# Summing u by channel block, and starting the channel MLP's first two feature groups side by side

## The chip, the cores and the metric

The kernel runs on one core of a Trainium2 chip. The metric is the device time of one execution in microseconds (us), as the median of several runs. A core has TensorE (matmuls), VectorE, ScalarE and GpSimd (elementwise work) and SyncE (which only issues DMAs here); each works through its own queue in order, and semaphores join the queues. In the rows they are PE (with PEld for the loading of weights), DVE, ACT, POOL and SP. TensorE writes into PSUM, eight banks of 512 float32 words per partition, which VectorE and ScalarE read.

## What is computed

Three stages follow one another: a gated linear attention, a mixing over the sequence with a channel MLP, and a second MLP with a spatial gate. The change lies at the start of the middle stage, for the first of four batches:

```python
def _moe_ref(x, U, V, w_ch1, w_ch2):          # x: (4, 768, 384)
    xt = x.transpose(0, 2, 1)
    h = xt @ U @ V                            # U: 768 x 32, V: 32 x 768
    u = x + h.transpose(0, 2, 1)
    ch = np.maximum(u @ w_ch1, 0.0) @ w_ch2   # 384 -> 1536 -> 384
    return (u + ch)
```

All is float32. Products run in a faster float32 mode on operands split into a high part and a low part (the rest): `high x high + low x high + high x low`.

## The kernel before

**Tiles.** A batch's u is held channels first: 384 channels are three blocks of 128 (index m or k, KE = 3), 768 positions are two blocks of 384 (index blk, NB = 2, TB = 384). A block's tuple is `(t, hi, lo)`: u in float32, its rounded copy and the rest. The 1536 hidden features are 12 groups of 128 (index f). A weight tile `w[f]` holds the high and the low parts of both matrices for one group.

**From x to u.** For each channel block m, `Mix.product` multiplies the transposed x with U into one PSUM bank, and `keep` writes it to columns m of `stk`: ScalarE copies 96 rows (line 1242), VectorE subtracts for the 32 rows of rests (line 1243). `mix_sum` then multiplies `stk` (block m) with V on TensorE (line 318), VectorE adds the result to t (line 322), ScalarE makes hi (line 323), and `rest` makes lo (line 252). In `first_batch` of the kernel before the order is: the three products with their keeps, `weights.add()`, all six sums with their hi copies, four products that fill time (`busy`, line 945), six rests (block 0, m = 0 on GpSimd, five on VectorE), and `weights.finish(1)`.

**The channel MLP.** For features 0 to 4 the two position blocks run side by side (`side_by_side`). The up product of a group and a block is nine matmuls (wh x uh, wh x ul, wl x uh, three channel blocks each, line 380) into a bank; ScalarE takes the ReLU to h (line 387, line 409 for the first group) and VectorE the rest hl = max(bank, 0) - h (`rest_of_h`, line 368). So the bank is read twice, and last by VectorE. `up_both` makes the first group for both blocks: six high products of block 0, six of block 1, then three low products of each (line 400). The down product (`down_group`, lines 287 to 289) is three times three matmuls into three accumulators; it runs two groups behind (`flush(2)`), so after the up products of (f0, block 0), (f0, block 1) and (f1, block 0) comes the down product of (f0, block 0), then the up product of (f1, block 1), then the down product of (f0, block 1). Within a down product the rest of the last h is put into VectorE's queue between the first and the second accumulator (`if m == 1: self.rest_of_h()`).

**Banks.** Banks are taken in turn by name: "acc" is banks 0 to 2, "mm" 3 and 4, "x" 5 to 7. Up products use "mm"; the accumulators of block 0 are three "acc", those of block 1 three "x"; the mixing products use "x"; the sums of u use "acc" for block 0 and "x" for block 1. A bank that is taken again waits for the last reader of what it held.

**Weights.** Features are loaded as 64-bit words and taken apart: two VectorE operations for the high word (lines 237 and 240), a scaling of the low word on ScalarE (line 232), an add of both (line 247, on GpSimd for features 0 and 1, on VectorE after them), a high part by ScalarE (line 791) and a low part by VectorE (line 252). These steps are spread by hand: `pull()` is called at fixed points of the MLP, and `FIRST_STEPS` says at which pull a step is queued ("f": the next half of the splitting, "b": the beginning of the next feature). At the 5th pull, inside `up_both`, the low part of f1 is queued; at the 6th feature 2 begins; at the 13th, inside the up product of (f1, block 1), "fbf" queues the high part of f2, the three operations of f3 and the low part of f2. The need for f1 (`need(2)`) queues the loads of pairs 5 and 6.

Of the kernel before, what the change touches and what calls it, by code (L numbers as in the profile page):

```python
# [36 lines left out]
F32 = mybir.dt.float32  # L37
# [3 lines left out]
AF = mybir.ActivationFunctionType  # L41
# [21 lines left out]
KE = E // 128  # L63
TB = 384
NB = S // TB
# [7 lines left out]
FIRST = (0, 5, 8, 10, 12)  # L73
# [27 lines left out]
def gla_mixer_gating_kernel(ctx: ExitStack, tc: tile.TileContext, akq, v, v2, vT, u, v3, w12, w_in, wsT, b_sp, w_out, out):  # L101
    nc = tc.nc
# [38 lines left out]
    class Stage:  # L141
# [38 lines left out]
        def high(self, room=None):  # L180

            place, words, t, n, wide, finish = self.loaded.pop(0)
            if wide and not place:
                t = (room or self.narrow())[0 : words.shape[0], 0:n]
            if wide:
                high_part(words, t)
            self.raised.append((place, words, t, wide, finish, self.scaled > 0))
            self.scaled = max(0, self.scaled - 1)
# [40 lines left out]
    def low_part(words):  # L229

        low = words.rearrange("p (n w) -> p n w", w=2)[:, :, 0]
        nc.scalar.activation(out=low, in_=low, func=AF.Copy, scale=2.0**-29)
# [17 lines left out]
    def rest(out, x, hi, engine=nc.gpsimd):  # L250

        engine.tensor_tensor(out=out, in0=x, in1=hi.bitcast(F32), op=ALU.subtract)  # L252
# [58 lines left out]
        )  # L311
        yield

    def mix_sum(g, block, blk, m, stk, psp, tag, engine=nc.gpsimd):

        t, hi, lo = block
        pt = psp.tile([128, 512], F32, "ps_h", tag)
        nc.tensor.matmul(
            out=pt[:, 0:TB], lhsT=stk[:, m * 128 : (m + 1) * 128], rhs=g["vs"][0 : stk.shape[0], blk * TB : (blk + 1) * TB],
            start=True, stop=True,  # L320
        )
        nc.vector.tensor_tensor(out=t[:, m, :], in0=pt[:, 0:TB], in1=t[:, m, :], op=ALU.add)
        nc.scalar.activation(out=hi[:, m, :], in_=t[:, m, :], func=AF.Copy)
        if engine:
            rest(lo[:, m, :], t[:, m, :], hi[:, m, :], engine)

    def mix_sum_steps(g, us, stk, up, psp, tag, blocks, parts=None):

# [7 lines left out]
    class ChannelMlp:  # L336
# [3 lines left out]
            self.wts, self.hp, self.psp, self.pull, self.need = wts, hp, psp, pull, need  # L340
            self.behind, self.h, self.accs, self.held = [], None, {}, False

        def side_by_side(self, b, blocks, f0, f1, tags):

            self.held = True
            for f in range(f0, f1):
                self.need(f + 1)
                for blk, h in enumerate(self.up_both(blocks, f) if f == f0 else (None, None)):
                    h = h or self.up_group(blocks[blk], f)
                    self.behind.append((b, blk, blocks[blk], f, h, f == f0, f == f1 - 1, tags[blk]))  # L350
                    self.flush(2)

# [16 lines left out]
                    out=hl, in0=ps[:, 0:TB], scalar=0.0, in1=h.bitcast(F32), op0=ALU.max, op1=ALU.subtract  # L369
                )  # L370

        def up_group(self, block, f):
            t, uh, ul = block
            w = self.wts
            ps = self.psp.tile([128, 512], F32, name="ps_1", tag="mm")

            wh, wl = w[f][:, 0], w[f][:, 1]
            parts = [(x, k) for x in ((wh, uh), (wh, ul), (wl, uh)) for k in range(KE)]
            for i, ((wx, ux), k) in enumerate(parts):
                nc.tensor.matmul(  # L380
                    out=ps[:, 0:TB], lhsT=wx[:, k * 128 : (k + 1) * 128], rhs=ux[:, k, :], start=i == 0, stop=i == len(parts) - 1
                )
                if i % 3 == 2 and i < len(parts) - 1:
                    self.pull()
            h = self.hp.tile([128, TB], F32R, name="h", tag="h", bufs=3)
            hl = self.hp.tile([128, TB], F32R, name="hl", tag="hl", bufs=3)
            nc.scalar.activation(out=h, in_=ps[:, 0:TB], func=AF.Relu)  # L387
            self.h = ps, h, hl
            return h, hl

        def up_both(self, blocks, f):
            w = self.wts
            wh, wl = w[f][:, 0], w[f][:, 1]
            both = [self.psp.tile([128, 512], F32, name="ps_1", tag="mm") for _ in blocks]

            for ends in (False, True):
                for (t, uh, ul), ps in zip(blocks, both):
                    parts = [(wh, ul, k) for k in range(KE)] if ends else [(wx, uh, k) for wx in (wh, wl) for k in range(KE)]
                    for i, (wx, ux, k) in enumerate(parts):
                        nc.tensor.matmul(  # L400
                            out=ps[:, 0:TB], lhsT=wx[:, k * 128 : (k + 1) * 128], rhs=ux[:, k, :],
                            start=i == 0 and not ends, stop=ends and i == KE - 1,
                        )
                    self.pull()
            hs = []
            for ps in both:
                h = self.hp.tile([128, TB], F32R, name="h", tag="h", bufs=3)
                hl = self.hp.tile([128, TB], F32R, name="hl", tag="hl", bufs=3)
                nc.scalar.activation(out=h, in_=ps[:, 0:TB], func=AF.Relu)
                self.h = ps, h, hl  # L410
                self.rest_of_h()
                hs.append((h, hl))
                if len(hs) == 1:
                    self.pull()
            return hs
# [391 lines left out]
    with ExitStack() as fast:  # L807
# [26 lines left out]
        ps = Ps(psp)  # L834
# [107 lines left out]
        def busy(n, bank):  # L942

            for _ in range(n):
                nc.tensor.matmul(out=bank[:, 512 - C : 512], lhsT=g["ident"], rhs=g["ident"], start=True, stop=True)

        class Pair:
# [77 lines left out]
            def keep(self):  # L1025

                after, self.w = self.after, states
                r0, r1 = slice(0, HW), slice(HW, 2 * HW)
                nc.scalar.activation(out=self.w[r0, :, 0, :], in_=after[r0, :, 0 : NCH - 1].rearrange("p e c -> p c e"), func=AF.Copy)
                nc.scalar.activation(out=self.w[r1, :, 1, :].rearrange("p c e -> p e c"), in_=after[r1, :, 0 : NCH - 1], func=AF.Copy)  # L1030
# [179 lines left out]
        class Mix:  # L1210
# [27 lines left out]
                return gp  # L1238

            def keep(self, gp):  # L1240
                o = slice(self.m * 128, (self.m + 1) * 128)
                nc.scalar.activation(out=self.stk[:, o], in_=gp[0 : 3 * R, 0:128], func=AF.Copy)
                nc.vector.tensor_tensor(
                    out=self.stk[R : 2 * R, o], in0=gp[R : 2 * R, 0:128], in1=self.stk[R : 2 * R, o].bitcast(F32), op=ALU.subtract
                )
# [157 lines left out]
        N_SMALL = 2  # L1403
# [12 lines left out]
        def first_batch(blocks):  # L1416
# [22 lines left out]
                mixes[m].take(pt[1], engine, room[1][:, m])  # L1439

            def summed(blk, m):
                mix_sum(g, blocks[blk], blk, m, stk, ps, ("acc", "x")[blk], None)

            for n in range(NP - 1):
                ahead = prepare(n + 1)
# [26 lines left out]
            narrow = [up.pool.tile([128, KE * TB], U32, name="narrow", tag=x) for x in ("uh0", "ul0")]  # L1472
            low_part(weights.loaded[0][1])
            low_part(weights.loaded[1][1])
            weights.scaled = N_SMALL + 1
            weights.high(narrow[0])
            weights.high(narrow[1])
            for _ in range(N_SMALL):
# [27 lines left out]
            weights.finish(1)  # L1506
            gp = mixes[1].product()
            mixes[1].keep(gp)
            blocks += [(us[blk], *up.parts()) for blk in range(NB)]
            gp = mixes[2].product()  # L1510
            mixes[2].keep(gp)
            weights.add()
            for blk, m in ((0, 0), (0, 1), (1, 0), (0, 2), (1, 1), (1, 2)):
                summed(blk, m)
            busy(4, ps.tile([128, 512], F32, "ps_w", "mm"))
            for blk in range(NB):
                t, hi, lo = blocks[blk]
                for m in range(KE):
                    rest(lo[:, m, :], t[:, m, :], hi[:, m, :], nc.gpsimd if blk == m == 0 else nc.vector)
            weights.finish(1)  # L1520
            yield
            load_pair(5)
            load_pair(6)
            next(ahead)
            yield

        blocks = []
        rest_of_first = first_batch(blocks)
        next(rest_of_first)
        nxt = []  # L1530
# [71 lines left out]
        for b in range(B):  # L1602
            if b == 0:
                n_steps = N_STEPS + N_AHEAD
            elif b + 1 < B:
                nxt = []
                steps, n_steps = attend(b + 1, nxt), N_STEPS + (2 if b > 0 else 0)
            else:
                ap_stack.close()
                gp = fast.enter_context(tc.tile_pool(name="gp", bufs=1, side="right"))  # L1610
                wts = gating_weights(gp)
                gating = Stage(gp, gating_items(wts), adders=range(NF1))
                steps = gating_steps()
            pulls, done = 0, 0
            groups = int(NB * NF1 * 2 * KE * (0.95 if b == 0 else 0.9))
            if b == 0:

                mlp.side_by_side(b, blocks, *FIRST[0:2], ("acc", "x"))
                for f0, f1 in zip(FIRST[1:-1], FIRST[2:]):
                    for blk in range(NB):  # L1620
                        mlp.block(b, blk, blocks[blk], f0, f1)
            else:
                for blk in range(NB):
                    mlp.block(b, blk, blocks[blk])
            drain(steps)
            blocks = nxt
# [184 lines left out]
```

## Time and profile before

| | us |
|---|---|
| median of 3 runs | 673.27 (673.02 to 673.37) |
| the profiled execution | 672.58 |
| its span, first to last instruction | 670.9 |
| TensorE busy | 657.1 (98%) |
| VectorE busy | 425.2 (63%) |
| ScalarE busy | 305.9 (46%) |
| GpSimd busy | 146.3 (22%) |

Times in the rows are from the start of the span. A row of the timeline is one instruction or several of one kind in a row (x and a number): start, length from the first's start to the last's end, engine, line, output and inputs, and in brackets the idle time of the engine before it with what ended it. Matmuls overlap, so a row of matmuls is longer than their spacing. The region of the change is 42 to 60 us.

### The profile page before, as it was taken

The numbers are of one execution on the slowest core, as the hardware profiler recorded it, in microseconds if no ns is written. First come the engines' busy times: TensorE is split into PE (matmuls) and PEld (weight loads), VectorE is DVE, ScalarE is ACT, GpSimd is POOL, SyncE is SP. The second block draws the span as 40 slices with busy tenths as digits, with TensorE's granted clock in tenths as the row PEclk, the third lists the DMA queues.
The fourth block names the chain that finished last, engine by engine and source line by source line (L and its number), as shares of the span: only waits on it lengthen the run. The fifth ranks groups of instructions, "written<-read, shape, count | busy, mean of one in ns | idle before, by whom it ended". The sixth has DMA issues, their size and how long they took to land.

```text
span 670.9 us, 13771 instructions
## 1 busy us (share of the span) xinstructions
PE 657.1 (98%) x5644; PEld 625.2 (93%) x5644; DVE 425.2 (63%) x813; ACT 305.9 (46%) x599; POOL 146.3 (22%) x138
## 2 busy tenths in 40 slices
PE   7999999999999999999999999999999999999996
PEld 6889999799999999999999999899999989999996
DVE  7989999867566336565327787586384356537541
ACT  3985467565455335554323444343344233334321
POOL 4530111133211131220120000306401620540041
PEclk9999999999999999999999999999999999999999
DMA  8799115562556502602023455401120202110011
GB/s 332 259 358 239 23 35 114 105 128 88 119 102 137 102 0 61 118 10 76 27 71 93 118 163 156 130 0 36 37 68 4 71 1 71 37 36 35 1 37 41
DMA packets 24039, 61.02 MB, mean 91 GB/s; under 512 B 3232, under 2 KB 13344, under 8 KB 22688
## 3 DMA queue, kind: packets, MB, share of 16 engines
q1 hardware_dynamic: 23968, 60.06, 32.7%
q8 instruction: 46, 0.75, 0.4%
q14 instruction: 25, 0.20, 0.1%
HBM read 47.47 MB, written 9.44 MB: 85 GB/s over the span
## 4 chain that ended last, share of the span: by engine, by line
PE 83%; DVE 11%; ACT 3%; issue 2%; DMA 0%; DVEq 0%; ACTq 0%
PE banks L380 19%; PE banks L287 18%; PE banks L288 18%; PE banks L289 18%; PE banks L1109 2%; DVE fw L933 2%; DVE bw L920 2%; PE banks L1008 1%; DVE narrow L240 1%; PE banks L980 1%; PE banks L964 1%; DVE narrow L247 1%; PE banks L1219 1%; DVE w L252 1%; PE banks L1235 1%
## 5 line engine op out<-in xcount | busy, mean ns | idle before, releaser
L380 PE MATMUL banks<-partuh,w 128*128 128x384 f32 x564 | 130.6, 339 | 1.4 <-DVE hl L368 1.2
L380 PEld LDWEIGHTS banks<-partuh,w 128*128 128x128 f32 x564 | 99.3, 188 | 3.1 <-DVE hl L368 1.8
L287 PE MATMUL banks<-h,w 128*128 128x384 f32 x288 | 98.0, 340 | 0.2
L289 PE MATMUL banks<-hl,w 128*128 128x384 f32 x288 | 96.4, 335 | 0.0
L288 PE MATMUL banks<-h,w 128*128 128x384 f32 x288 | 96.4, 335 | 0.0
L368 DVE SCALAR_TENSOR_TENSOR hl<-banks,h 128x384 fp32r<-128x384 f32 x96 | 52.7, 549 | 52.8 <-ACT h L387 52.2
L387 ACT ACTIVATE h<-banks 128x384 fp32r<-128x384 f32 x94 | 45.6, 487 | 76.9 <-PE banks L380 76.7
L252 POOL TENSOR_TENSOR partul<-ub,partuh 128x384 fp32r<-128x384 f32 x43 | 43.2, 1029 | 136.5 <-ACT partuh L457 84.1
L252 POOL TENSOR_TENSOR room<-room 128x384 fp32r<-128x384 f32 x32 | 32.5, 1017 | 163.5 <-ACT room L600 163.2
L380 PE MATMUL banks<-partul,w 128*128 128x384 f32 x282 | 66.0, 341 | 0.0
L287 PEld LDWEIGHTS banks<-h,w 128*128 128x128 f32 x288 | 54.0, 188 | 1.6 <-issue 0.8
L288 PEld LDWEIGHTS banks<-h,w 128*128 128x128 f32 x288 | 54.1, 188 | 0.0
L289 PEld LDWEIGHTS banks<-hl,w 128*128 128x128 f32 x288 | 54.1, 188 | 0.0
L909 POOL TENSOR_TENSOR akq<-akq,fw 128x768 f32<-128x768 f32 x13 | 22.5, 1731 | 135.0 <-DVE fw L933 86.6
L380 PEld LDWEIGHTS banks<-partul,w 128*128 128x128 f32 x282 | 49.2, 188 | 0.8
L600 ACT ACTIVATE room<-room 128x384 fp32r<-128x384 f32 x32 | 16.8, 525 | 66.8 <-DVE room L598 66.8
L252 DVE TENSOR_TENSOR vl<-vt,vh 128x512 fp32r<-128x512 f32 (+1 forms) x48 | 26.6, 616 | 20.7 <-ACT vh L505 20.7
L909 POOL TENSOR_TENSOR akq<-akq,bw 128x768 f32<-128x768 f32 x11 | 18.6, 1688 | 65.1 <-DVE bw L920 65.1
L288 PE MATMUL banks<-partuh,winl 128*128 128x384 f32 x96 | 32.4, 338 | 0.0
L289 PE MATMUL banks<-partul,winh 128*128 128x384 f32 x96 | 32.4, 338 | 0.0
L287 PE MATMUL banks<-partuh,winh 128*128 128x384 f32 x96 | 32.4, 338 | 0.0
L289 PE MATMUL banks<-woutl,room 128*128 128x384 f32 x96 | 32.3, 336 | 0.0
(256 smaller groups left out, 1495.9 us busy)
## 6 DMA issues: line engine op xcount, KB each, us to landing
akq<-in_akq SPq DMA_DIRECT2D x24, 434.4 KB, 7.5
bits<-in_w SPq DMA_DIRECT2D x12, 768.0 KB, 11.3
x2d<-ub SPq DMA_DIRECT2D x8, 576.0 KB, 3.3
ub<-x2d SPq DMA_DIRECT2D x8, 576.0 KB, 4.2
out_y<-room SPq DMA_DIRECT2D x24, 192.0 KB, 1.9
v<-in_v SPq DMA_DIRECT2D x15, 288.0 KB, 8.1
words<-in_wsT SPq DMA_DIRECT2D x7, 576.0 KB, 3.9
words<-in_w_in SPq DMA_DIRECT2D x8, 384.0 KB, 3.2
```

Of the source, the lines that this page charges most:

```text
L252: engine.tensor_tensor(out=out, in0=x, in1=hi.bitcast(F32), op=ALU.subtract)
L287: nc.tensor.matmul(out=ps, lhsT=wh, rhs=xh, start=first, stop=False, skip_group_check=more)
L288: nc.tensor.matmul(out=ps, lhsT=wl, rhs=xh, start=False, stop=False, skip_group_check=more)
L289: nc.tensor.matmul(out=ps, lhsT=wh, rhs=xl, start=False, stop=last, skip_group_check=more)
L368: nc.vector.scalar_tensor_tensor(out=hl, in0=ps[:, 0:TB], scalar=0.0, in1=h.bitcast(F32), op0=ALU.max, op1=ALU.subtract)
L380: nc.tensor.matmul(out=ps[:, 0:TB], lhsT=wx[:, k * 128 : (k + 1) * 128], rhs=ux[:, k, :], start=i == 0, stop=i == len(parts) - 1)
L387: nc.scalar.activation(out=h, in_=ps[:, 0:TB], func=AF.Relu)
L600: nc.scalar.activation(out=hi, in_=x, func=AF.Copy)
L909: engine.tensor_tensor(out=chunks(x)[:, c], in0=chunks(x)[:, c], in1=chunks(by)[:, c, 1:CW], op=ALU.mult)
L920: nc.vector.tensor_tensor_scan(out=bw[:, ::-1], data0=a[:, 1 : AW + 1][:, ::-1], data1=ends[:, ::-1], initial=0.0, op0=ALU.mult, op1=ALU.max)
L933: nc.vector.tensor_tensor_scan(out=fw, data0=a[:, 0:AW], data1=starts, initial=0.0, op0=ALU.mult, op1=ALU.max)
L1109: nc.tensor.matmul(out=self.py[HW * h : HW * h + D, x, j * CH : (j + 1) * CH], lhsT=vw[:, h, c, :], rhs=self.sms[h][:, t], start=True, sto ...
```

## The change

The sums of u are split into their steps (`mix_add`, `raised` for hi, `lowered` for lo). In `first_batch` the scaling and the add for feature 1 move ahead; the sums for channel block 0 of both position blocks are queued ahead of the third mixing product, and those for block 1 behind it, around the two halves of its keep. The sums for channel block 2, their hi copies, the splitting of feature 1's high part and five rests become `last_sums`, which `up_both` calls after its first two matmuls. `up_both` goes by channel block, high and low weights of each, and between the low products of block 0 and of block 1 it makes the first three matmuls (wh x uh) of feature 1 for both position blocks, into two more banks, named "x"; `up_group` for feature 1 then adds the other six. The four products that filled time are gone.

```diff
+    def mix_add(g, block, blk, m, stk, psp, tag):
+        t = block[0]
         pt = psp.tile([128, 512], F32, "ps_h", tag)
...
         nc.vector.tensor_tensor(out=t[:, m, :], in0=pt[:, 0:TB], in1=t[:, m, :], op=ALU.add)
...
-                for blk, h in enumerate(self.up_both(blocks, f) if f == f0 else (None, None)):
-                    h = h or self.up_group(blocks[blk], f)
+                hs, begun = [None] * NB, [None] * NB
+                if f == f0:
+                    hs = self.up_both(blocks, f, last_sums)
+                elif f == f0 + 1:
+                    begun = self.begun
+                for blk in range(NB):
+                    h = hs[blk] or self.up_group(blocks[blk], f, begun[blk])
...
-        def up_group(self, block, f):
+        def up_group(self, block, f, begun=None):
...
-            ps = self.psp.tile([128, 512], F32, name="ps_1", tag="mm")
+            ps = begun or self.psp.tile([128, 512], F32, name="ps_1", tag="mm")
...
+                if i >= KE or not begun:
...
+        def up_both(self, blocks, f, last_sums):
+            both, self.begun = ([self.psp.tile([128, 512], F32, name="ps_1", tag=x) for _ in blocks] for x in ("mm", "x"))
...
+            high(0, 0)
+            last_sums()
+            high(1, 0)
+            for k in range(1, KE):
+                for blk in range(NB):
+                    high(blk, k)
+                self.pull()
+            low(0)
+            self.pull()
+            for blk in range(NB):
+                for k in range(KE):
+                    nc.tensor.matmul(
+                        out=self.begun[blk][:, 0:TB], lhsT=self.wts[f + 1][:, 0, k * 128 : (k + 1) * 128], rhs=blocks[blk][1][:, k, :],
+                        start=k == 0, stop=False,
+                    )
+            low(1)
+            self.pull()
...
             mixes[1].keep(gp)
+            low_part(weights.raised[0][1])
+            weights.add()
             blocks += [(us[blk], *up.parts()) for blk in range(NB)]
+            summed(0, 0)
+            summed(1, 0)
             gp = mixes[2].product()
-            mixes[2].keep(gp)
-            weights.add()
-            for blk, m in ((0, 0), (0, 1), (1, 0), (0, 2), (1, 1), (1, 2)):
-                summed(blk, m)
-            busy(4, ps.tile([128, 512], F32, "ps_w", "mm"))
...
+            raised(0, 0)
+            mixes[2].keep_high(gp)
+            summed(0, 1)
+            mixes[2].keep_rest(gp)
+            summed(1, 1)
+            lowered(0, 0)
+            for blk, m in ((1, 0), (0, 1), (1, 1)):
+                raised(blk, m)
+
+            def last_sums():
+                for blk in range(NB):
+                    summed(blk, KE - 1)
+                for blk in range(NB):
+                    raised(blk, KE - 1)
+                weights.finish(1)
+                for blk, m in ((0, 1), (0, 2), (1, 0), (1, 1), (1, 2)):
+                    lowered(blk, m)
+
+            junction.append(last_sums)
             yield
```

## Rows read from the trace of the kernel before

**Rows 1.** The page's totals: busy us, share of the span, instructions of each engine
```profile
PE 657.1 (98%) x5644; PEld 625.2 (93%) x5644; DVE 425.2 (63%) x813; ACT 305.9 (46%) x599; POOL 146.3 (22%) x138
```

**Rows 2.** Busy us (instructions) of each engine by stretch, then clock, DMA share, GB/s
```profile
59.40:122.50 63.10, 61.09 (x768) 56.78 (x766) 62.01 (x99) 36.95 (x65) 5.09 (x3) 1.00 0.43 82
128.00:665.00 537.00, 536.54 (x4152) 517.16 (x4149) 307.24 (x633) 223.09 (x443) 117.68 (x107) 1.00 0.26 69
```

**Rows 3.** VectorE's waits from 43.9 to 122.5 us: total, times, longest
```profile
DVE hl L368 <- ACT h L387: 0.9, 1, 0.9
```

**Rows 4.** The chain of waits, 50 to 175 us: start, length, what
```profile
57.19 0.88 DVE w L252
58.12 0.81 PE banks L380 x3
58.95 0.50 ACT h L387
...
127.05 0.29 DVE stk L1243
127.48 0.85 PE banks L964 x6
```

**Rows 5.** The timeline of VectorE, 41 to 60 us
```profile
42.70 0.28 DVE L1243 TENSOR_TENSOR stk<-banks,stk 32x128 fp32r<-32x128 f32 x1
43.81 0.28 DVE L1243 TENSOR_TENSOR stk<-banks,stk 32x128 fp32r<-32x128 f32 x1 [0.83 <-ACT stk L1242]
44.13 2.88 DVE L322 TENSOR_TENSOR ub<-banks,ub 128x384 f32<-128x384 f32 x6
46.93 2.84 DVE L252 TENSOR_TENSOR partul<-ub,partuh 128x384 fp32r<-128x384 f32 x5
49.83 0.56 DVE L368 SCALAR_TENSOR_TENSOR hl<-banks,h 128x384 fp32r<-128x384 f32 x1
...
51.17 0.55 DVE L368 SCALAR_TENSOR_TENSOR hl<-banks,h 128x384 fp32r<-128x384 f32 x1
...
54.19 0.55 DVE L368 SCALAR_TENSOR_TENSOR hl<-banks,h 128x384 fp32r<-128x384 f32 x1
...
57.98 0.55 DVE L368 SCALAR_TENSOR_TENSOR hl<-banks,h 128x384 fp32r<-128x384 f32 x1
59.47 0.56 DVE L368 SCALAR_TENSOR_TENSOR hl<-banks,h 128x384 fp32r<-128x384 f32 x1 [0.94 <-ACT h L387]
```

**Rows 6.** Line 252 from 46 to 50 us: shortest, median, longest in ns
```profile
L252 DVE TENSOR_TENSOR partul<-ub,partuh x5: 544/544/967, 46.9 to 49.2; 128x384 fp32r<-128x384 f32 x5
```

**Rows 7.** The timeline of GpSimd, 41 to 60 us
```profile
44.65 1.86 POOL L247 TENSOR_TENSOR narrow<-narrow,bits 128x768 uint32<-128x768 uint32 x1 [5.99 <-ACT bits L232]
46.47 1.01 POOL L252 TENSOR_TENSOR partul<-ub,partuh 128x384 fp32r<-128x384 f32 x1
```

**Rows 8.** The timeline of ScalarE, 41 to 60 us
```profile
43.68 0.89 ACT L232 ACTIVATE bits<-bits 128x768 uint32<-128x768 uint32 x1
44.77 2.80 ACT L323 ACTIVATE partuh<-ub 128x384 fp32r<-128x384 f32 x6 [0.19 <-ACT bits L232]
```

**Rows 9.** The timeline of TensorE, 43 to 60 us
```profile
44.78 1.05 PE L945 MATMUL banks<-ident 128*128 128x128 f32 x8
...
46.74 2.01 PE L400 MATMUL banks<-partuh,w 128*128 128x384 f32 x10 [0.53 <-ACT partuh L323]
...
50.44 0.79 PE L380 MATMUL banks<-partuh,w 128*128 128x384 f32 x3 [0.18 <-DVE hl L368]
...
56.79 0.68 PE L380 MATMUL banks<-partuh,w 128*128 128x384 f32 x3
57.31 0.68 PE L380 MATMUL banks<-partul,w 128*128 128x384 f32 x3
```

**Rows 10.** TensorE's first matmuls, and the stretch behind its last one (clock 0.93)
```profile
1.43 4.43 PE L945 MATMUL banks<-ident 128*128 128x128 f32 x24 [1.43 <-POOL ident masks.py:199]
...
666.00:670.90 4.90, 0.00 (x0) 0.00 (x0) 0.00 (x0) 0.00 (x0) 0.00 (x0) 0.93 0.16 50
```

More of the change, by code (lines that the diff above doesn't have):

```diff
@@ L312, in mix_tile_steps @@
         yield
-    def mix_sum(g, block, blk, m, stk, psp, tag, engine=nc.gpsimd):
-        t, hi, lo = block
+    def mix_add(g, block, blk, m, stk, psp, tag):
+        t = block[0]
         pt = psp.tile([128, 512], F32, "ps_h", tag)
@@ L322, in mix_sum @@
         nc.vector.tensor_tensor(out=t[:, m, :], in0=pt[:, 0:TB], in1=t[:, m, :], op=ALU.add)
+    def mix_sum(g, block, blk, m, stk, psp, tag):
+        t, hi, lo = block
+        mix_add(g, block, blk, m, stk, psp, tag)
         nc.scalar.activation(out=hi[:, m, :], in_=t[:, m, :], func=AF.Copy)
-        if engine:
-            rest(lo[:, m, :], t[:, m, :], hi[:, m, :], engine)
+        rest(lo[:, m, :], t[:, m, :], hi[:, m, :])
     def mix_sum_steps(g, us, stk, up, psp, tag, blocks, parts=None):
@@ L341, in __init__, with side_by_side @@
             self.behind, self.h, self.accs, self.held = [], None, {}, False
-        def side_by_side(self, b, blocks, f0, f1, tags):
+        def side_by_side(self, b, blocks, f0, f1, tags, last_sums):
             self.held = True
@@ L379, in up_group @@
             for i, ((wx, ux), k) in enumerate(parts):
-                nc.tensor.matmul(
-                    out=ps[:, 0:TB], lhsT=wx[:, k * 128 : (k + 1) * 128], rhs=ux[:, k, :], start=i == 0, stop=i == len(parts) - 1
-                )
+                if i >= KE or not begun:
+                    nc.tensor.matmul(
+                        out=ps[:, 0:TB], lhsT=wx[:, k * 128 : (k + 1) * 128], rhs=ux[:, k, :], start=i == 0, stop=i == len(parts) - 1
+                    )
                 if i % 3 == 2 and i < len(parts) - 1:
@@ L389, in up_group, with high, low @@
             return h, hl
[L391 to L404, printed above, removed]
+        def up_both(self, blocks, f, last_sums):
+            both, self.begun = ([self.psp.tile([128, 512], F32, name="ps_1", tag=x) for _ in blocks] for x in ("mm", "x"))
+            def high(blk, k):
+                for i in range(2):
+                    nc.tensor.matmul(
+                        out=both[blk][:, 0:TB], lhsT=self.wts[f][:, i, k * 128 : (k + 1) * 128], rhs=blocks[blk][1][:, k, :],
+                        start=k == i == 0, stop=False,
+                    )
+            def low(blk):
+                for k in range(KE):
+                    nc.tensor.matmul(
+                        out=both[blk][:, 0:TB], lhsT=self.wts[f][:, 0, k * 128 : (k + 1) * 128], rhs=blocks[blk][2][:, k, :],
+                        start=False, stop=k == KE - 1,
+                    )
+            high(0, 0)
[8 more added lines that the diff above has]
+            for blk in range(NB):
+                for k in range(KE):
+                    nc.tensor.matmul(
+                        out=self.begun[blk][:, 0:TB], lhsT=self.wts[f + 1][:, 0, k * 128 : (k + 1) * 128], rhs=blocks[blk][1][:, k, :],
+                        start=k == 0, stop=False,
+                    )
+            low(1)
+            self.pull()
             hs = []
@@ L1240, in keep, with keep_high, keep_rest @@
             def keep(self, gp):
+                self.keep_high(gp)
+                self.keep_rest(gp)
+            def keep_high(self, gp):
                 o = slice(self.m * 128, (self.m + 1) * 128)
                 nc.scalar.activation(out=self.stk[:, o], in_=gp[0 : 3 * R, 0:128], func=AF.Copy)
+            def keep_rest(self, gp):
+                o = slice(self.m * 128, (self.m + 1) * 128)
                 nc.vector.tensor_tensor(
@@ L1441, in summed, with raised, lowered @@
             def summed(blk, m):
-                mix_sum(g, blocks[blk], blk, m, stk, ps, ("acc", "x")[blk], None)
+                mix_add(g, blocks[blk], blk, m, stk, ps, ("acc", "x")[blk])
+            def raised(blk, m):
+                t, hi, lo = blocks[blk]
+                nc.scalar.activation(out=hi[:, m, :], in_=t[:, m, :], func=AF.Copy)
+            def lowered(blk, m):
+                t, hi, lo = blocks[blk]
+                rest(lo[:, m, :], t[:, m, :], hi[:, m, :], nc.gpsimd if blk == m == 0 else nc.vector)
             for n in range(NP - 1):
@@ L1474, in first_batch @@
             low_part(weights.loaded[1][1])
-            weights.scaled = N_SMALL + 1
+            weights.scaled = N_SMALL + 2
             weights.high(narrow[0])
@@ L1508, in first_batch @@
             mixes[1].keep(gp)
+            low_part(weights.raised[0][1])
+            weights.add()
             blocks += [(us[blk], *up.parts()) for blk in range(NB)]
+            summed(0, 0)
+            summed(1, 0)
             gp = mixes[2].product()
-            mixes[2].keep(gp)
-            weights.add()
-            for blk, m in ((0, 0), (0, 1), (1, 0), (0, 2), (1, 1), (1, 2)):
-                summed(blk, m)
-            busy(4, ps.tile([128, 512], F32, "ps_w", "mm"))
[L1516 to L1520, printed above, removed]
+            raised(0, 0)
[15 more added lines that the diff above has]
+            junction.append(last_sums)
             yield
@@ L1525, in first_batch @@
             yield
-        blocks = []
+        blocks, junction = [], []
         rest_of_first = first_batch(blocks)
@@ L1616, in gla_mixer_gating_kernel @@
             if b == 0:
-                mlp.side_by_side(b, blocks, *FIRST[0:2], ("acc", "x"))
+                mlp.side_by_side(b, blocks, *FIRST[0:2], ("acc", "x"), junction.pop())
                 for f0, f1 in zip(FIRST[1:-1], FIRST[2:]):
```

## The prediction

> **What bounds the kernel now.** I read the engine totals first: TensorE is busy for 98% of the span, VectorE for 63% [rows 1]. Shares of the whole span say little about one place, so I cut the span into stretches. From 128 us on TensorE is busy 536.54 of 537.00 us: nothing there can take up a delay or add to a gain, and whatever stands at 128 us is carried to the end. Between 59.4 and 122.5 us it is VectorE that never rests: 62.01 of 63.10 us [rows 2]. Its list of waits from 43.9 to 122.5 us has only one on another engine after the sums, 0.9 us for one ReLU [rows 3]. The chain of waits says where these two meet: at 58.07 us the low half of feature group 2's weights is done, TensorE goes on 0.05 later, and the ReLU of that group follows at 58.95; at 127.48 TensorE goes on again right behind a VectorE operation [rows 4]. So the question for this change is one number: how much earlier or later VectorE begins the rest of h of group 2, block 0, which stands at 59.47 us now [rows 5]. Everything behind that is a queue without idle time, on VectorE first and on TensorE then, and shifts as a whole.
>
> I write f0, f1, f2 for feature groups and b0, b1 for blocks.
>
> **Part 1, the sums.** Now VectorE idles 0.83 us ahead of the last rest for stk (43.81), since the third product is summed before anything else is added; six adds take 2.80 from 44.13 to 46.93; five rests of u take 2.77 up to 49.70; then come hl of f0 b0 (49.83), f1's low weights and hl of f0 b1 (51.17) [rows 5]. In the new order:
> The first two sums need only the first block of stk and go ahead of the third product. The first add can follow the rest at 42.70 as closely as 44.13 follows 43.81, by 0.32: 43.02, which is 1.11 earlier. But that third rest (0.32) now lies between the adds. The add of (0,1) must wait for its matmul behind the third product, an estimated 0.09. The sum of (1,2) gets the bank of (1,1), because two of the three banks "x" are by then set aside for the begun products of f1; it waits for that add, about 0.12. So the adds end at 43.02 + 2.80 + 0.32 + 0.21 = 46.35, against 46.93: of 1.11 us, 0.58 are left.
> The five rests: their rows read 0.544 us for most and 0.967 for one [rows 6], the first, which ran while GpSimd's rest (46.47 to 47.48) did [rows 7]. GpSimd's add for f1 waits now for ScalarE's scaling at 43.68 [rows 8]; this moves ahead of the third product, behind the second keep, whose rest stands at 42.70, so to about 42.4, and GpSimd's two operations (1.86 and 1.01) end near 46.2, before the first rest of VectorE. Five at 0.47 each from 46.35 end at 48.70, 1.00 earlier than now.
> The Trainium skill has the rule for it (SBUF — State Buffer, section "Who interferes with whom"): a VectorE instruction with two SBUF inputs and a GpSimd instruction that reads SBUF exclude each other, and the adds, with one input in PSUM, are exempt. The trace agrees: the six adds ran under GpSimd's 1.86 us at one pace, 2.80 for all, the first rest did not keep its 0.544. Without that rule the first rest would stay at 0.97, and the sum below would be 1.86 instead of 1.72.
>
> **Part 2, the first products.** TensorE takes f0 by channel block, so it starts before the last sums, but its last pair of high products needs the copy of u (1,2), whose add ends at 46.45; the copy, about half a us (six in 2.80 [rows 8]), ends at 47.02. From 47.10 come two products, three of b0's low part, six begun ones of f1 and three of b1's low part, 0.173 apart (a group of three is 0.52 behind the last [rows 9]), 0.28 behind the first after a wait: the last one starts at 49.46 and ends at 49.79. f1's high weights, next on ScalarE behind that copy, are there at about 47.8, ahead of the begun six at 48.07. The six begun products are only moved, they take TensorE time that it lost before to waits (0.53 us at 46.74, 0.18 at 50.44 [rows 9]); they delay b1's ReLU by 1.04 us where it might have come sooner. ReLU 0.49, and hl of f0 b1 starts at 50.35 instead of 51.17. So up to here VectorE is **0.82 us** ahead. Bounds: VectorE's own queue without a single wait would have it 1.36 ahead (43.02, six adds, 0.32, five rests, hl 0.47, weights 0.87: 49.81); if half of the waits above are twice as long, 0.5.
> The four idle-filling products (1.05 us, eight rows [rows 9]) lie in a wait of TensorE and cost nothing when removed; the wait behind them was for a copy of u. ScalarE's scaling, moved, ends near 43.3, before the third product does (43.83), so the keep behind it waits for nothing new; without that cover it would cost 0.9. No DMA is moved: the loads of pairs 5 and 6 stay at the need for f1. The pulls of the first group stay five, so every step of the list by pulls keeps its place in the queues of ScalarE and VectorE.
>
> **Part 3, the banks.** This is where I expect the loss. Block 1's three accumulators take the three banks "x" in turn, the next after begun f1 b0, begun f1 b1, sum (1,2): so accumulator 0 falls on the bank of f1 b0, **accumulator 1 on the bank of f1 b1**. That bank is read by the ReLU and by hl of f1 b1. The first down product of b1 (f0) comes right behind the up product of f1 b1, and hl of f1 b1 stands in VectorE's queue behind all that the 13th pull puts there: f3's three operations and f2's low weights. In the trace it runs at 57.98, 6.81 us after hl of f0 b1 [rows 5], and all of that is in between still. So it starts at 50.35 + 6.81 = 57.16, ends at 57.71, and TensorE may write accumulator 1 at 57.77. Today these accumulators find free banks, and f1's h in the two "mm" banks is not written over until f2. That TensorE does wait for such a read is in the trace: the up product of f1 b0 at 50.44 stood 0.18 for the hl of f0 b0 on the same bank [rows 9].
> TensorE gets there much sooner: f1 b0's six remaining products end at 51.06 (its low weights are ready at 50.2), down f0 b0 nine, up f1 b1 six, then accumulator 0 from 53.98 (it waits for hl of f1 b0, 53.92): it is done with it at 54.8 and stands for some **3 us**. Behind the wait are queued two thirds of that down product (6 matmuls) and the up product of f2 b0 (9), which before were almost done by then. Fifteen matmuls after a stall take 0.81 + 4 × 0.52 = 2.89 us [rows 4, 9]: 57.77 + 2.89 = 60.66 for the end of f2 b0, against 58.93. VectorE has nothing to do meanwhile, because the next thing in its queue is hl of f2 b0. So this hl comes 1.73 later.
> In one line: the end of f2 b0 is 58.53 + 0.05 + 2.89 = 61.47 less what VectorE gains up to hl of f1 b1, against 58.93 now: **shift = 2.54 − gain**. With 0.82 it is +1.72 us; with the bounds 1.36 and 0.5, +1.2 to +2.0. There is no way for the gain to reach 2.54: VectorE's queue alone allows 1.36.
>
> **Sum.** The profiled execution spans 670.9 us and took 672.58, 0.69 below the median of the runs, 673.27. Shifted: 674.3 for such an execution, **675.0** for the median. A measurement of this kernel can tell about 0.2%, 1.35 us, from no change.
>
> **Rivals.**
> (a) The bank wait does not decide (the accumulators find other banks, or hl of f1 b1 is out before 54.8). Then TensorE arrives early at f2's low weights, which VectorE ends 0.82 sooner than 58.07, and all shifts by −0.8: **672.45**, not slower. For it: the wait can't be seen in the trace of before, it follows from counting banks. Against: the count leaves no other bank, and it decides as soon as f3's three operations stand ahead of that hl.
> (b) The delay is partly given back. VectorE idles 1.09 of 63.10 us up to 122.5 [rows 2]; if all of it were slack, +0.6 would be left: **673.9**. Against: the list of waits [rows 3] shows none of them as a wait for another engine; gaps between dependent operations stay.
> (c) TensorE's clock falls in the new idle stretch. The granted clock was at its upper level (2.4 GHz, 1.00) through all waits of the body; behind the last matmul it fell only late in the stretch of 666 to 670.9 us without work (mean 0.93) [rows 10]. Getting back cost about 1.6 us at the start: 24 products in 4.43 us [rows 10], where eight take 1.05 later [rows 9], about 0.111 apart with a tail of 0.16, so that 24 would take 2.83. Result 675.0 + 1.6 = **676.6**. Against: the wait here is some 3 us, shorter than the stretch at the end in which the level held at first.
> The Trainium skill (TensorE: Matmul & The Clock Gate, section "Why this matters for your kernels") warns against leaving TensorE idle between bursts of matmuls, since the clock can go back to its half rate. By that rule (c) would be the result; the trace of before has no idle stretch of such a length inside the body, so it can't say.
>
> **How the numbers follow.** Forecast 0.66, (a) 0.13, (b) 0.13, (c) 0.08. Of the forecast's range (674.5 to 675.3) nearly all lies above 674.62, the bound for slower; some 0.1 may be just below. Slower: 0.56 + 0.08 = 0.64; within: 0.10 + 0.13 + 0.08 = 0.31; faster only if (a) comes with twice the gain: 0.05. The range 673.3 to 676.2 takes in the forecast with its bounds and (b); (a) and (c) stay out.
>
> **What would show it.** In the changed profile: the first add of u starts near 43.0; TensorE has one wait of about 3 us between 54 and 58 us, on a down product of h, ended by VectorE's hl; VectorE idles some 3.4 us ahead of the next hl near 61.2; from there every operation stands 1.7 us later, to the end. I am wrong if that wait is under 1 us, if it is ended by something else, or if hl of f2 b0 starts before 60 us.

## The result

| | median us | ratio to before (95%) | profiled execution, span |
|---|---|---|---|
| before | 673.10 | | 672.58, 670.9 |
| after | 676.62 | 1.0054 (1.0044 to 1.0064) | 675.94, 674.2 |

The change makes the kernel slower by 3.5 us, 0.5%. The forecast was 675.0, with a range of 673.3 to 676.2: the direction is right, the size is half of what came, and the time lies outside the range. It is the time of rival (c), 676.6.

The totals hardly move (TensorE's busy time grows by 1.6 us, against [rows 1]):

```profile
PE 658.7 (98%) x5636; PEld 626.5 (93%) x5636; DVE 424.4 (63%) x813; ACT 306.5 (45%) x599; POOL 146.2 (22%) x138
```

VectorE from 41 to 66 us, the lines that answer to [rows 5]:

```profile
42.63 0.28 DVE L1281 TENSOR_TENSOR stk<-banks,stk 32x128 fp32r<-32x128 f32 x1
42.95 1.59 DVE L322 TENSOR_TENSOR ub<-banks,ub 128x384 f32<-128x384 f32 x3
44.57 0.28 DVE L1281 TENSOR_TENSOR stk<-banks,stk 32x128 fp32r<-32x128 f32 x1
44.89 1.65 DVE L322 TENSOR_TENSOR ub<-banks,ub 128x384 f32<-128x384 f32 x3
46.45 2.42 DVE L252 TENSOR_TENSOR partul<-ub,partuh 128x384 fp32r<-128x384 f32 x5
...
50.41 0.56 DVE L377 SCALAR_TENSOR_TENSOR hl<-banks,h 128x384 fp32r<-128x384 f32 x1
...
53.44 0.55 DVE L377 SCALAR_TENSOR_TENSOR hl<-banks,h 128x384 fp32r<-128x384 f32 x1
...
57.23 0.55 DVE L377 SCALAR_TENSOR_TENSOR hl<-banks,h 128x384 fp32r<-128x384 f32 x1
62.84 0.56 DVE L377 SCALAR_TENSOR_TENSOR hl<-banks,h 128x384 fp32r<-128x384 f32 x1 [5.05 <-ACT h L397]
```

The first add stands at 42.95 instead of 44.13, the rests of u at 46.45 instead of 46.93 and no longer with a slow one among them (against [rows 6]; GpSimd's own rest, the second line, is done at 46.14):

```profile
L252 DVE TENSOR_TENSOR partul<-ub,partuh x5: 548/552/553, 46.5 to 48.3; 128x384 fp32r<-128x384 f32 x5
45.13 1.01 POOL L252 TENSOR_TENSOR partul<-ub,partuh 128x384 fp32r<-128x384 f32 x1
```

hl of f0 b1 stands at 50.41 (before: 51.17), hl of f1 b1 at 57.23 (57.98): VectorE is 0.75 us ahead, as long as it depends on itself. Then it idles for 5.05 us, and hl of f2 b0 comes at 62.84 instead of 59.47, 3.37 later. TensorE in the same stretch:

```profile
54.05 0.44 PE L287 MATMUL banks<-h,w 128*128 128x384 f32 x1 [0.29 <-DVE hl L377]
...
54.51 0.33 PE L289 MATMUL banks<-hl,w 128*128 128x384 f32 x1
57.84 0.44 PE L287 MATMUL banks<-h,w 128*128 128x384 f32 x1 [3.00 <-DVE hl L377]
...
58.62 0.52 PE L287 MATMUL banks<-h,w 128*128 128x384 f32 x1
...
61.50 0.77 PE L390 MATMUL banks<-partuh,w 128*128 128x384 f32 x3
62.11 0.33 PE L287 MATMUL banks<-h,w 128*128 128x384 f32 x1
```

It makes the first accumulator of block 1 (54.05 to 54.51; 0.29 of waiting for the bank of f1 b0), then stands for 3.00 us until hl of f1 b1 has left the bank of the second one. Behind that wait the spacing of its matmuls does not stay at 0.173: from 58.62 on, nine matmuls take 2.88 up to 61.50, 0.320 each. The windows show why (in each line the third number from the end is the granted clock):

```profile
53.80:57.80 4.00, 0.79 (x3) 0.47 (x3) 3.92 (x6) 1.77 (x3) 0.00 (x0) 1.00 1.11 365
58.30:61.60 3.30, 3.30 (x12) 3.30 (x12) 0.00 (x0) 0.00 (x0) 0.00 (x0) 0.50 1.01 198
```

From 53.80 to 57.80 us it is 1.00, though TensorE works for 0.79 us only; from 58.30 to 61.60 it is 0.50, the lower level, 1.2 GHz. It is still 1.00 up to 58.25, so here the clock falls only after the matmuls have begun again. The fifteen matmuls behind the wait take 4.43 us, from 57.84 to 61.50 + 0.77 = 62.27; the prediction had 2.89. The chain of waits of the changed kernel, against [rows 4], runs from hl of f1 b1 through 15 matmuls to the ReLU of f2 b0, and the shift of 3.3 us is still there at 130 us (130.74 against 127.48):

```profile
57.32 0.48 DVE hl L377
57.84 0.44 PE banks L287
...
59.78 2.50 PE banks L390 x9
62.31 0.50 ACT h L397
...
130.31 0.30 DVE stk L1281
130.74 0.85 PE banks L995 x6
```

The same shift stands at the end of the span, 674.2 against 670.9.

### The profile page after: what moved, and what is told of

Same layout as the page of the kernel before. It is cut to its first block, busy times and chain, and to the rows that moved or that the text cites. A ratio compares the mean times of both kernels' runs of the same rounds, so it can differ in the third digit from the quotient of the medians.

```text
span 674.2 us, 13756 instructions
## 1 busy us (share of the span) xinstructions
PE 658.7 (98%) x5636; PEld 626.5 (93%) x5636; DVE 424.4 (63%) x813; ACT 306.5 (45%) x599; POOL 146.2 (22%) x138
## 4 chain that ended last, share of the span: by engine, by line
PE 81%; DVE 13%; DMA 2%; issue 2%; ACT 2%; SPq 1%; DVEq 0%; ACTq 0%
PE banks L390 19%; PE banks L287 18%; PE banks L289 18%; PE banks L288 18%; PE banks L1140 2%; DVE bw L951 2%; DVE fw L964 2%; DVE narrow L240 1%; DMA bits<-in_w 1%; DVE hl L377 1%; PE banks L1011 1%; PE banks L1039 1%; DVE narrow L247 1%; DVE w L252 1%; PE banks L995 1%
```

## The experiments

Each kernel was timed against the kernel before on the same chip. The first four shared one set of runs of before (median 673.02), the last four another (672.84). None leaves out a part of the computation.

| kernel | median us | against before | ratio (95%) |
|---|---|---|---|
| wait filled with idle products | 674.58 | +1.56 | 1.0024 (1.0014 to 1.0035) |
| rest of h ahead of the 13th pull's steps | 672.91 | -0.11 | 0.9999 (0.9990 to 1.0008) |
| no begun products | 671.75 | -1.27 | 0.9985 (0.9976 to 0.9994) |
| begun products for block 0 alone | 671.66 | -1.36 | 0.9979 (0.9970 to 0.9988) |
| before, with the banks alone | 677.41 | +4.57 | 1.0054 (1.0040 to 1.0068) |
| wait at the third accumulator | 675.24 | +2.40 | 1.0030 (1.0019 to 1.0042) |
| block 0 alone, f2 ahead of f3 | 671.09 | -1.75 | 0.9970 (0.9959 to 0.9982) |
| before, f2 ahead of f3 | 672.70 | -0.14 | 0.9998 (0.9988 to 1.0007) |

**1. The wait filled.** This parts the clock from the wait.

```diff
                 if m == 1:
                     self.rest_of_h()
+                    if begin and blk == 1 and self.held:
+                        self.fill()
...
+        mlp.fill = lambda: busy(12, ps.banks[:, PLACES["mm"][1], :])
```

The bank is one of the two "mm", which nothing holds at that time; each of the twelve products is two rows of the trace.

> The changed kernel with twelve idle-filling products (128 columns each, about 2.7 us) queued between the first and the second accumulator of the first down product of block 1, into a bank that is free there. Theory (the bank wait costs about 1.75 us, and the fall of TensorE's clock behind it another 1.6): TensorE still reaches the second accumulator at about 57.8, but the granted clock stays at 1.00, the end of feature group 2's up product for block 0 comes at 60.7 instead of 62.3, and the time is about 674.9 (1.7 above before, not 3.5). Rival (the clock's fall is hidden, since VectorE bounds what follows, and the whole loss is the wait): no change, 676.6.

TensorE's rows, the window, and hl of f2 b0, after the edit:

```profile
54.75 2.84 PE L978 MATMUL banks<-ident 128*128 128x128 f32 x24
57.91 0.45 PE L287 MATMUL banks<-h,w 128*128 128x384 f32 x1 [0.32 <-DVE hl L377]
...
60.12 0.68 PE L390 MATMUL banks<-partuh,w 128*128 128x384 f32 x3
```

```profile
57.90:61.70 3.80, 3.79 (x22) 3.79 (x23) 0.33 (x1) 0.86 (x2) 0.00 (x0) 1.00 0.99 169
61.37 0.56 DVE L377 SCALAR_TENSOR_TENSOR hl<-banks,h 128x384 fp32r<-128x384 f32 x1 [3.51 <-ACT h L397]
```

The products fill the wait but for 0.32 us, and the second accumulator still begins where VectorE lets it, at 57.91. The clock holds, and the 15 matmuls end at 60.12 + 0.68 = 60.80: 2.89 us behind their start, the very sum of the prediction. hl of f2 b0 comes at 61.37, 1.90 later than before the change and 1.47 sooner than in the changed kernel. So the clock's fall costs about 1.5 us in the profiled executions (2.0 between the medians), and the wait without it 1.6 to 1.9. Added work made the changed kernel 2 us faster.

**2. The rest of h ahead.** This takes the wait's cause away and leaves banks and products.

```diff
-    5: "f", 6: "b", 13: "fbf", 22: "fbf", ...
+    5: "f", 6: "b", 16: "fbf", 22: "fbf", ...
```

> The changed kernel with the steps of the 13th pull (high part of f2, three operations of f3, low part of f2) queued at the 16th pull, which lies behind the rest of h of f1, block 1; banks and products as in the changed kernel. Theory (the wait for the bank, set by VectorE's order, decides): that rest runs near 54.4 instead of 57.2, the wait of TensorE falls from 3.0 us to about 0.3, the clock stays at 1.00, the low part of f2 ends near 58.2 as it does before the change, and the time is within 0.5 us of before (672.7 to 673.5). Rival (the loss comes from the new order of sums and products itself): 676 or more.

```profile
54.37 0.56 DVE L377 SCALAR_TENSOR_TENSOR hl<-banks,h 128x384 fp32r<-128x384 f32 x1 [0.29 <-ACT h L397]
...
59.66 0.56 DVE L377 SCALAR_TENSOR_TENSOR hl<-banks,h 128x384 fp32r<-128x384 f32 x1 [1.41 <-ACT h L397]
```

```profile
54.99 0.45 PE L287 MATMUL banks<-h,w 128*128 128x384 f32 x1
...
58.31 0.79 PE L390 MATMUL banks<-partuh,w 128*128 128x384 f32 x3 [0.94 <-DVE w L252]
```

hl of f1 b1 runs at 54.37 instead of 57.23, as soon as its ReLU is there, and the second accumulator begins at 54.99. The time is that of before. It wins nothing because f3's operations and f2's low weights come later by as much: TensorE now waits 0.94 us for these at 58.31 (0.05 behind them, as in [rows 4], only 0.2 later than there). So the loss of the change is not in the new order of sums. It takes two things together: the new bank, and the place of this one rest of h in VectorE's queue. The kernel before has that queue with other banks, this run has the banks with another queue, and neither has the wait of 3 us.

**3. No begun products.** Sums by channel block and the first group's order stay; f1 is made whole, in its old banks.

```diff
-            both, self.begun = ([...tile(..., tag=x) for _ in blocks] for x in ("mm", "x"))
+            both, self.begun = [...tile(..., tag="mm") for _ in blocks], [None] * NB
...
-            for blk in range(NB):
-                for k in range(KE):
-                    nc.tensor.matmul(out=self.begun[blk][:, 0:TB], ...)
```

> The changed kernel without the six begun products of f1: nine are made at their usual place, into the two banks that they had before the change. Sums by channel block and the first group's order stay. Theory (banks): no wait of TensorE on a rest of h at a down product, clock 1.00, VectorE some 0.9 us ahead at the low part of f2 (57.1 instead of 58.06), and that decides: 672.2. Rival (the early sums and their order cost the time): 675 or more.

```profile
57.07 0.55 DVE L377 SCALAR_TENSOR_TENSOR hl<-banks,h 128x384 fp32r<-128x384 f32 x1
58.55 0.56 DVE L377 SCALAR_TENSOR_TENSOR hl<-banks,h 128x384 fp32r<-128x384 f32 x1 [0.94 <-ACT h L397]
```

No wait of TensorE on a rest of h is left between 44 and 64 us. VectorE's rows have the shape of [rows 5], hl of f1 b1 and then 0.94 us of idle time, but 0.91 earlier. The shift of -0.91 stays through 400 us. The time is 1.27 below before, where 0.9 was expected; the span of the profiled execution gives 1.0 (669.9).

**4. Begun for block 0 alone.** Three begun products instead of six, f1 b1 in its bank "mm".

```diff
-            both, self.begun = ([...tile(..., tag=x) for _ in blocks] for x in ("mm", "x"))
+            both = [...tile(..., tag="mm") for _ in blocks]
+            self.begun = [...tile(..., tag="x"), None]
...
-            for blk in range(NB):
+            for blk in range(1):
                 for k in range(KE):
                     nc.tensor.matmul(out=self.begun[blk][:, 0:TB], ...)
```

> The changed kernel with three begun products of f1, for block 0 alone; f1 of block 1 is made in its usual bank. The accumulators of block 1 then meet the bank of f1, block 0, as the third of them, whose rest of h is long out. Theory (only the bank of f1, block 1, hurts): no wait of 3 us, clock 1.00, 672.3. Rival (a begun product in an accumulator's bank hurts in any block): a wait of about a us remains, 674 to 675.

The bank of f1 b0 is met by the second accumulator, not by the third as the expectation says; that changes nothing, as its rest is out by 53.75.

```profile
50.30 0.79 PE L390 MATMUL banks<-partuh,w 128*128 128x384 f32 x3 [0.43 <-DVE w L252]
...
57.12 0.81 PE L390 MATMUL banks<-partuh,w 128*128 128x384 f32 x3 [0.30 <-DVE w L252]
```

TensorE, having got ahead, waits instead for weights: 0.43 us for f1's low part, 0.30 for f2's, each set by VectorE. The time is 671.66, under the 672.3 expected; no wait of TensorE on a rest of h is left. So the three begun products win nothing that these runs can tell: 671.66 with them, 671.75 without any. What is worth something in the change is the rest, the sums and the first group by channel block.

**5. Before, with the banks alone.** f1's up products into banks "x", turned as the changed kernel has them, and nothing else.

```diff
-            ps = self.psp.tile([128, 512], F32, name="ps_1", tag="mm")
+            ps = self.psp.tile([128, 512], F32, name="ps_1", tag="x" if self.held and f == 1 else "mm")
...
+                if blk == 1 and self.held:
+                    self.psp.place("x")
                 self.accs[blk] = [...]
```

> The kernel before the change, with one thing of the change alone: the up products of f1 go into banks x, turned so that the accumulators of block 1 meet them as in the changed kernel (block 0 first, block 1 second). Sums, order and all products as before. Theory (bank wait by itself): TensorE reaches the second accumulator near 55.9, waits for the rest of h of f1, block 1 (58.53), some 2.7 us; nothing was gained earlier, so the shift is the full 2.5 us: 675.6 if the clock stays, 677.1 if it falls in the wait. Rival (the wait is a thing of the early sums): 673.0.

```profile
55.34 0.34 PE L289 MATMUL banks<-hl,w 128*128 128x384 f32 x1
58.53 0.69 PE L287 MATMUL banks<-h,w 128*128 128x384 f32 x1 [2.85 <-DVE hl L368]
...
59.65 0.53 PE L287 MATMUL banks<-h,w 128*128 128x384 f32 x1
```

```profile
58.53:61.40 2.87, 2.87 (x9) 2.87 (x10) 0.00 (x0) 0.00 (x0) 0.00 (x0) 0.50 0.91 166
```

The wait arises in the old order as well, 2.85 us, ended by the same operation (line 368), and the clock is at 0.50 behind it. With nothing gained beforehand the whole is worse than the change itself. Its five executions fall into two groups: three with a mean clock of 0.992 to 0.996 took 677.41 to 677.77 us, two with 0.998 and 0.999 took 676.12 and 675.38. These two are 3.28 and 2.54 above before; the prediction's figure for a wait without any gain and without a fall of the clock is 2.54, so that one of the two meets it and the other is 0.7 over it, for which no trace was kept. (The profiled execution, one of the three, lost another 0.95 at 413 us, waiting for a load of the next stage.)

**6. The wait at the third accumulator.** The banks "x" are turned by two more places, so that fewer matmuls stand behind the wait.

```diff
+                if blk == 1 and self.held:
+                    self.psp.place("x"), self.psp.place("x")
                 self.accs[blk] = [...]
```

> The changed kernel with the banks x turned by two before block 1's accumulators are taken: the bank of f1, block 0, is met by the second, that of f1, block 1, by the third accumulator. Theory: the wait ends at the same 57.8, set by VectorE, but only 12 matmuls stand behind it instead of 15; with the clock falling in the wait as in the changed kernel, the end of f2's up product of block 0 comes some 0.5 us sooner: about 676.1; with the clock kept at its upper level, 674.5. Rival (the wait's length and not what is queued behind it counts): 676.6, or a little less than that by the shorter wait.

```profile
57.97 0.44 PE L287 MATMUL banks<-h,w 128*128 128x384 f32 x1 [2.99 <-DVE hl L377]
...
58.59 0.98 PE L390 MATMUL banks<-partuh,w 128*128 128x384 f32 x3
...
60.33 1.16 PE L390 MATMUL banks<-partuh,w 128*128 128x384 f32 x3
62.05 0.56 DVE L377 SCALAR_TENSOR_TENSOR hl<-banks,h 128x384 fp32r<-128x384 f32 x1 [4.14 <-ACT h L397]
```

The wait has the same length, 2.99 us, and ends 0.13 later. What comes behind is shorter by a third of a down product: from the wait's end to the end of f2 b0 it is 3.52 us (57.97 to 61.49), not 4.43, and hl of f2 b0 is 2.59 later than before the change, not 3.37. That is more than the 0.5 expected: three matmuls less at the lower clock are 0.96, not 0.52. The median, 675.24, is under the 676.1 expected for it. The one execution of seven with a mean clock of 0.999 took 673.74, the others 674.86 to 675.70. So with a wait of one length the loss goes by the work that is queued behind it.

**7. and 8. f2 ahead of f3.** If VectorE's idle time ahead of hl of f2 b0 is what bounds the stage, then less of it is time won. At the 13th pull both halves of f2's splitting go ahead of f3's operations, once on top of experiment 4, once on the kernel before.

```diff
-    ... 13: "fbf", ...
+    ... 13: "ffb", ...
```

> The kernel with three begun products for block 0 alone, and at the 13th pull both halves of f2's splitting queued ahead of f3's three operations. Theory (VectorE's idle time ahead of the rest of h of f2, block 0, now 0.96 us, is what is left to win, since VectorE hardly rests from there to 122 us): the low part of f2 comes near 55.0 instead of 57.1, TensorE does not wait for it, VectorE idles about 0.5 us once, waiting for ScalarE's high part, and that rest of h starts near 57.8: 671.0. Rival (f3's operations, which come later, are waited for instead): 671.6 or more.

> The kernel before the change with only the 13th pull's steps turned: both halves of f2's splitting ahead of f3's operations. Theory (VectorE's idle time decides): its 0.94 us ahead of the rest of h of f2, block 0, turn into some 0.5 ahead of the low part of f2: 672.4 to 672.6. Rival (that idle time is hidden by TensorE's own work): 673.0.

VectorE in the first of them, then in the second:

```profile
54.01 0.96 DVE L252 TENSOR_TENSOR w<-narrow,w 128x768 fp32r<-128x768 f32 x1 [0.45 <-ACT w L823]
...
57.35 1.01 DVE L377 SCALAR_TENSOR_TENSOR hl<-banks,h 128x384 fp32r<-128x384 f32 x2
```

```profile
55.12 0.96 DVE L252 TENSOR_TENSOR w<-narrow,w 128x768 fp32r<-128x768 f32 x1 [0.45 <-ACT w L791]
...
58.46 1.11 DVE L368 SCALAR_TENSOR_TENSOR hl<-banks,h 128x384 fp32r<-128x384 f32 x2
```

In both VectorE idles 0.45 us ahead of f2's low weights, and hl of f1 b1 and of f2 b0 then follow each other without a gap (x2). With experiment 4's kernel under it the time is 1.75 us below before, 0.3%, the lowest median here; from experiment 4 itself, 1.36 below, it is not told apart, as the two intervals overlap. On the kernel before, hl of f2 b0 is 0.46 earlier in the profile, and 0.43 of it hold up to 390 us; at 413 us VectorE waits 2.59 us for a load of the next stage instead of 2.21, and 0.2 is left. The medians differ by 0.14, within the interval: the mechanism shows in the trace, a gain in the time does not.

## Why the prediction was half right

**The sums** (part 1): right. First add 42.95 (forecast 43.02), rests of u from 46.45 (46.35), hl of f0 b1 at 50.41 (50.35), VectorE 0.75 us ahead (0.82). With GpSimd's two operations over before the rests begin, the longest rest takes 0.553 instead of 0.967; in the two runs that keep the old order of the sums (experiments 5 and 8), the five rests still average 0.633 and 0.635, against 0.551 here. The Trainium skill (SBUF — State Buffer, section "Who interferes with whom") says that a VectorE instruction with two SBUF inputs contends with a GpSimd instruction that reads SBUF; these numbers agree.

**The banks** (part 3): right, and shown. The wait is where it was counted out, 3.00 us long ("some 3"), ended by hl of f1 b1 at 57.84 (57.77). Experiment 5 makes it with the banks alone, experiment 2 takes its cause away, and experiment 1, where the clock stays up, times what is behind it: 2.89.

**No slack behind** (the first part): right. VectorE's 62.01 of 63.10 us meant that next to nothing is given back: the shift of hl of f2 b0, 3.37, is 3.26 at 130 us and 3.3 at the end. Rival (b) falls; so does (a), since the wait decides. That whatever stands at 128 us is carried to the end is not quite so: at 413 us, where VectorE waits for a load of the next stage, experiment 5 lost another 0.95 and experiment 8 some 0.2 of its 0.43.

**The clock**: this is the step that failed. The sum took its last term, fifteen matmuls behind the wait, at the upper level, 2.89 us, and put the fall of the clock at nothing; with the fall the term measured 4.43. The prediction had the fall as rival (c), with a price near the right one (1.6; measured 1.5 between the two profiles) and the right time, but gave it a chance of 0.08, by this argument: the wait is "shorter than the stretch at the end in which the level held at first". That row says only that the level once held for some time behind the last matmul, some 4.9 us there. It is one sample from one place and no lower bound: in experiment 6 the level had fallen 2.0 us behind the last matmul, which ends at 667.78.

```profile
667.80:669.70 1.90, 0.00 (x0) 0.00 (x0) 0.00 (x0) 0.49 (x1) 0.00 (x0) 1.00 0.48 163
669.80:673.30 3.50, 0.00 (x0) 0.00 (x0) 0.00 (x0) 0.00 (x0) 0.00 (x0) 0.50 0.04 10
```

The price was in part luck: the first 24 products, from which it was taken, took 4.43 us in the profile of before but 5.49 in that of the changed kernel, and the same working gives 2.7 from that row. The fall is seen in the profiled execution; the changed kernel's six executions all have a mean clock of 0.992 to 0.996, where those of before have 0.997 to 1.000, so that it most likely came in each of them. The Trainium skill (TensorE: Matmul & The Clock Gate, section "Why this matters for your kernels"), by which TensorE left idle between bursts of matmuls can fall back to half its clock, spoke against the forecast; this run agrees, with 0.50 behind 3.00 idle us. The fall was set beside the forecast like another course of things, but it is a consequence of the forecast's own wait: it belonged in the sum, or at least inside the range.

**The begun products** (part 2): their place was right, their worth not looked at. The prediction called them moved work; experiments 3 and 4 show that the three of block 0 are worth nothing that can be measured, as TensorE then waits for weights that VectorE makes. All six were never run with neither the bank wait nor a later start of f3's operations, so what they would be worth there is not shown. That the change without them is a gain, 1.3 us, stood in the prediction only as the time of rival (a), 0.8 below before.

## What to carry to other kernels

A matmul that is begun early needs a bank longer; find out which later product takes that bank next, and what stands in the reader's queue ahead of the operation that sets it free. Where one engine never rests for the next 60 us, a wait of another engine is paid for in the work that is queued behind it, and an early start of the second engine bought nothing here. And a new idle stretch of TensorE of some 3 us, as in these runs, is to be priced with a fall of its clock behind it; filling it with idle products recovered 2 us.

## What the runs showed that I had not expected

Executions of the changed kernel differ among themselves: with a mean clock of 0.996 it took 675.94 to 676.38 us, with 0.994 and 0.992 676.85 to 677.32. The profile kept is of one of the first kind. The mean clock also counts the idle time behind the last matmul, where the level falls too ([rows 10]), and no profile of the slower executions was kept; whether the clock was low for longer there, or fell a second time, is not shown.

By their mean clock two executions of five show no such fall in experiment 5 (wait of 2.85 us in the profiled one), and one of seven in experiment 6 (2.99). What decides that stays open.
